# Layer 2 of eight blocks by seven products instead of eight

## The chip, the cores and the metric

The kernel runs on one core of a Trainium2 chip. The metric is the device time of one execution in microseconds; the kernel before takes 678.67 us, the median of three runs (678.66 to 679.11). The engines of the core are TensorE (PE in the profile, with its weight loads as PEld), VectorE (DVE), ScalarE (ACT), GpSimd (POOL) and SyncE (SP, which here only issues DMAs).

## The reference

```python
# x: 8 x 4096 x 192, weight: 8 heads x 7 taps, w_in: 192 x 2048, w_out: 2048 x 192
w = softmax(weight, axis=-1)                       # one set of 7 taps for each head of 24 channels
y[b, s, c] = sum(w[head(c), k] * x[b, s + k - 6, c] for k in range(7))   # zeros before the start
h = y.reshape(32768, 192) @ w_in                   # layer 1
out = gelu_exact(h) @ w_out                        # layer 2
```

Inputs and output are float32. Both layers have 192 x 2048 weights and 32768 tokens.

## The kernel before

**Tiling.** The tokens are split into two halves of 16384. A block n takes the same stretch of both halves: 256 tokens of each in blocks 0 to 5, 512 of each in blocks 6 to 34 (`WS`, `TB`, `NB` = 35). `M0` = 6 and `M1` = 34 bound the blocks whose layer 2 is made transposed (`mm2_t`, L821).

**Convolution.** VectorE transposes a block's input from `xin` to `xT` (`trans`, L493), and `conv` (L518) makes seven taps in fourteen instructions, each tap once for two thirds of the channels (1024 elements a partition) and once for the last third (512). The first tap is a multiplication (L537), the others multiply and add into `acc` (L544), and the last writes bf16 into `xc`. Three blocks, 4, 5 and 6 (`K0`), have their first tap made by ScalarE in three instructions (`first_tap`, L640, with semaphore `S_K0`); for them the transpose stands earlier, inside the convolution of the block before. GpSimd copies the last six tokens of a block to the front of the next (`halo`, L430).

**TensorE.** Each block n has sixteen units. A unit is `mm1(n, i)`, twelve matmuls of layer 1 into one of two PSUM buffers `hp`, and then a share of layer 2 of block n - 1. All matmuls in the blocks from 7 on use a 64x64 quarter of the array; four run side by side, and four of 512 columns are called a round here. `mm1` has 3 rounds a unit, 48 a block. `mm2_t` has three passes over the sixteen chunks of 128 hidden features, 48 rounds; every pass fills parts of the three PSUM banks of a block's output thirds (output column c belongs to third c mod 3). The shares are written by hand:

```python
SHARE = [3, 3, 3, 3, 4, 3, 3, 3, 3, 4, 3, 3, 3, 3, 2, 2]
```

The four banks of `ob` are used in turn (`ring`, L333). Waits on TensorE hold up everything queued after them.

**ScalarE** makes one gelu of 128 x 1024 a unit (L674), from `hp` to `gT`, and `mm1` of unit u waits until the gelu of unit u - 2 is done.

**VectorE's order** is a written list. `plan` holds, for each block, the convolution's instructions; `side` holds everything else with a place (block, position) in that plan. So far these are the transposes of layer 2's banks to `osb` (`evac_t`, L336), three a block, the first after pass 1 of layer 2 and two after its end. Plan n runs roughly while TensorE is in block n - 1.

**DMA.** SP issues the load of block n + 3, then the store of block n - 1, in turns; the load waits for `trans` of the block whose buffer it takes, the store for the third `evac_t`.

Of the kernel before, what the change touches and what calls it, by code (L numbers as in the profile page):

```python
# [5 lines left out]
ALU = mybir.AluOpType  # L6
AF = mybir.ActivationFunctionType
BF16 = mybir.dt.bfloat16
# [3 lines left out]
def bass_lightweight_conv__then__act_gelu_exact_kernel(  # L12
# [19 lines left out]

    WS = [256] * 6 + [512] * ((HALF - 1536) // 512)
    PC = {0: 0, 1: 1}

    K0 = {4: 0, 5: 1, 6: 2}

    NA = 5
    NB = len(WS)
# [31 lines left out]


    M0, M1 = 6, NB - 1

    PHC, MMC, EVC = [0], [0], [0]
    for n in range(NB):
        new = M0 <= n < M1
        PHC.append(PHC[n] + (2 if new else 3 * NG[n] if n == 0 else NG[n]))
        MMC.append(MMC[n] + (1 if new else 2 * NG[n] if n == M1 else NG[n]))
        EVC.append(EVC[n] + (0 if n < NA else NP if new else NG[n]))  # L80

# [3 lines left out]

    CG = [[0, 1, 4, 5, 2, 6, 3, 7], [1, 0, 5, 4, 2, 6, 3, 7]]
    CH = [[2 * CG[hf][i // 2] + i % 2 for i in range(NF)] for hf in range(2)]
    assert all(WS[n] == TB for n in range(M0, NB)) and NG[NB - 1] == 4 and SL0[NB] % 2 == 0

    OUTS = []  # L90
# [6 lines left out]
    def sbt(name, shape, dt):  # L97
        return es.enter_context(nc.sbuf_tensor(name, shape, dt))
# [10 lines left out]
    with es:  # L109
# [17 lines left out]
        xc = [sbt("xc%d" % i, [128, NP * TB], BF16) for i in range(2)]  # L127
        gT = [sbt("gT%d" % i, [128, NF * 2 * TB], BF16) for i in range(2)]
        osb = [sbt("osb%d" % i, [128, 8 * C], F32) for i in range(2)]
        hp = [pst("hp%d" % i, [128, 2 * TB]) for i in range(2)]  # L130
        ob = pst("ob", [128, 2048])

# [28 lines left out]
        S_EVA = sem("S_EVA")  # L161
        S_EVB = sem("S_EVB")
        S_K0 = sem("S_K0")

        block = es.enter_context(nc.Block())

# [97 lines left out]
        def banks(m, g):  # L264


            if m < M0:
                return [bank(2 * ((G0[m] + g) % 2) + h, w=C) for h in range(2)]
            if g % 2:
                return [hp[g // 2][:, h * TB : h * TB + C] for h in range(2)]  # L270
            r = NP * (M1 - 1 - M0)
            return [bank(b, w=C) for b in sorted((b % 4 for b in ((r + 3, r), (r + 1, r + 2))[g // 2]))]

        def wait_ev(e, m, g):

# [54 lines left out]

        UPLO = [(1, 0), (0, 2), (2, 1)]

        def ring(m, j):  # L333
            return NP * (m - M0) + j

        def evac_t(v, m, j):  # L336

            if j == 0:
                v.wait_ge(S_PH, PHC[m] + 2)
                v.wait_ge(S_OUT[m % 2], OUTS[m - 2])  # L340
            else:
                v.wait_ge(S_MM2, MMC[m + 1])
            v.transpose(  # L343
                ap(osb[m % 2], j, [[8 * C, 128], [C // 2, TB // 32], [NP, 32]]),
                bank(ring(m, j)),
            ).then_inc(S_EV)

        def load(e, n, qs=(0, 2, 1, 3), sm=None):
            mb = WS[n] // 32
# [10 lines left out]
        def store(e, m):  # L360
            if m < M0:
                for g in range(NG[m]):
                    wait_ev(e, m, g)
                    e.dma_start(
                        ap(
                            outt,
                            (OFF[m] + 128 * g) * C,
                            [[C, 128], [HALF * C, 2], [1, C]],
                        ),
                        ap(osb[m % 2], g * C, [[8 * C, 128], [4 * C, 2], [1, C]]),  # L370
                    ).then_inc(S_OUT[m % 2], 16)
                return
            wait_ev(e, m, NP - 1)
            for q in range(4):

                e.dma_start(
                    ap(
                        outt,
                        ((q // 2) * HALF + OFF[m]) * C + (q % 2) * (C // 2),
                        [[C, 32], [32 * C, WS[m] // 32], [1, C // 2]],  # L380
                    ),
                    ap(
                        osb[m % 2],
                        32 * q * 8 * C,
                        [[8 * C, 32], [C // 2, WS[m] // 32], [1, C // 2]],
                    ),
                ).then_inc(S_OUT[m % 2], 16)

        @block.gpsimd
        def _(g):  # L390
# [76 lines left out]
        def _(v):  # L467
# [84 lines left out]
            for n in range(2, NB):  # L552
                ops = [] if n in K0 else [("t", n, 0)]
                ops += [("c", n, k, q) for k in range(int(n in K0), KS) for q in range(2)]
                if n + 1 in K0:
                    ops[6:6] = [("t", n + 1, 0)]
                plan.append(ops)

            def run(op):
# [20 lines left out]
            for j in range(3, len(pieces(1))):  # L580
                conv_out(v, 1, j)

            side = [((M0 + 2, 4 * g), evac, v, M0 - 1, g) for g in range(NG[M0 - 1])]
            for n in range(M0, M1):
                for j, at in enumerate([(n + 2, 12), (n + 3, 4), (n + 3, 6)]):
                    side.append((at, evac_t, v, n, j))
            for n in range(M1, NB):
                for g in range(NG[n]):
                    side.append(((n + 3, g), evac_half, v, g, 0))
            side.sort(key=lambda q: q[0])  # L590
            for b in range(2, NB):
                for o, op in enumerate(plan[b - 2]):
                    while side and side[0][0] <= (b, o):
                        side[0][1](*side[0][2:])
                        side.pop(0)
                    run(op)
# [4 lines left out]
        def _(a):  # L601
# [31 lines left out]
                due[m + 2, 0] = [(m, 1)]  # L633

            first = {}
            for n, at in ((4, (3, 5, 6)), (5, (3, 5, 6)), (6, (2, 3, 5))):
                for p in range(NP):
                    first[n - 2, at[p]] = (n, p)

# [12 lines left out]
            for n in range(NB):  # L652
                w = WS[n]
                for i in range(NSL[n]):
                    u = SL0[n] + i
                    c = NCH[n]
                    if (n, i) in first:
                        first_tap(*first[n, i])
                    if (n, i) == (0, 4):
                        conv_out(a, 1, 0)  # L660
                    for k in due.get((n, i), []):
                        evac(a, *k)
                    a.wait_ge(S_MM1, u + 1)
                    if i == 0 and n >= 2:
                        a.wait_ge(S_MM2, MMC[n - 1])
                    if M0 <= n < M1:

                        src = [[2 * TB, 128], [1, 2 * TB]]
                        dst = [[NF * 2 * TB, 128], [1, 2 * TB]]
                    else:  # L670

                        src = [[2 * TB, 128], [TB, 2], [128, 4], [1, 128]]
                        dst = [[NF * 2 * TB, 128], [128, 2], [256, 4], [1, 128]]
                    a.activation(  # L674
                        out=ap(gT[n % 2], i * c * 2 * w, dst),
                        in_=ap(ob, 2 * TB, [[4 * TB, 128], *src[1:]]) if u < SL0[1] and u % 3 == 2 else ap(hp[u % 3 if u < SL0[1] else u % 2], 0, src),
                        func=AF.Gelu,
                    ).then_inc(S_GELU)
# [6 lines left out]
        def _(t):  # L685
# [43 lines left out]
            def mm1(n, i):  # L729
# [22 lines left out]
                for cc, p in todo:  # L752
# [4 lines left out]
                            t.wait_ge(S_CV, cvd(n))  # L757
                    for hf in range(2):
                        r = slice(64 * hf, 64 * hf + 64)
                        ch = CH[hf][i * c + cc]  # L760
                        f0 = FQ * ((ch // 2) ^ hf) + ch % 2
                        fw = 64 if (n == 0 and 4 <= i <= 5) or M0 < n <= M1 else 128
                        for fo in range(0, 128, fw):
# [57 lines left out]
            def mm2_t(m, ps, i):  # L821

                w = WS[m]
                if i == 0:
                    if ps < 2:
                        t.wait_ge(S_EV, EVC[m] - (1 if m == M0 else 2) + ps)
                    if ps > 0:
                        t.wait_ge(S_PH, PHC[m] + ps)
# [3 lines left out]
                for hf in range(2):  # L832
                    j = UPLO[ps][hf]
                    r = slice(64 * hf, 64 * hf + 64)
                    for h in range(2):
                        c0 = (2 * i + h) * w
                        ins = t.matmul(  # L837
                            bank(ring(m, j), slice(64 * h, 64 * h + 64), w),
                            ap(
                                wout,  # L840
                                64 * hf * NF * C + CH[h][i] * C + j,
# [8 lines left out]
                    ins.then_inc(S_MM2 if ps == 2 else S_PH)  # L850


            SHARE = [3, 3, 3, 3, 4, 3, 3, 3, 3, 4, 3, 3, 3, 3, 2, 2]

            def units(m):
                if M0 <= m < M1:
                    return [(ps, i) for ps in range(3) for i in range(NF)]
                return [
                    (g, ph, i) for g in range(NG[m]) for ph in range(2) for i in range(NF)
                ]  # L860
# [3 lines left out]
            for n in range(NB):  # L864
# [4 lines left out]
                for i in range(NSL[n]):  # L869
                    mm1(n, i)  # L870
                    for q in behind.get((n, i), []):
                        pconv(*q)
                    new = M0 < n <= M1
                    ws = SHARE if new else [0] * 7 + [1] if n == 0 else [1] * NSL[n]
                    a0 = len(todo) * sum(ws[:i]) // sum(ws)
                    a1 = len(todo) * sum(ws[: i + 1]) // sum(ws)
                    for un in todo[a0:a1]:
                        if n < 2 and un[:2] == (0, int(un[2] // 4 == 1)) and un[2] % 4 == 0:
                            t.wait_ge(S_WOUT[un[2] // 4], 16)
                        (mm2_t if new else mm2)(max(n - 1, 0), *un)  # L880
            m = NB - 1
            for g in range(NG[m]):
                wait_banks(t, m, g)
# [59 lines left out]
```

## Time and profile before

| what | value |
|---|---|
| runs | 679.11, 678.67, 678.66 us; median 678.67 |
| profiled execution, first to last instruction (span) | 676.8 us |
| median of the runs less that span | 1.87 us |
| mean granted TensorE clock | 1.000 |
| gelu L674, mean | 1023 ns, 510 times |
| matmuls of layer 1 and 2, 64x64 with 512 columns | 5376 each, 376 ns each, four side by side |
| convolution tap L544, 1024 and 512 elements, mean | 1272 and 714 ns |
| bank transpose L343, input transpose L516 of 1536 | 888 and 2316 ns |

The profile shows one execution. Durations of neighbours on an engine overlap a little, so the distance between two starts is shorter than a duration. The execution's own time is taken as its span; the runs' median lies 1.87 us above it.

### The profile page before, as it was taken

The numbers are of one execution on the slowest core, as the hardware profiler recorded it, in microseconds if no ns is written. First come the engines' busy times: TensorE is split into PE (matmuls) and PEld (weight loads), VectorE is DVE, ScalarE is ACT, GpSimd is POOL, SyncE is SP. The second block draws the span as 40 slices with busy tenths as digits, with TensorE's granted clock in tenths as the row PEclk, the third lists the DMA queues.
The fourth block names the chain that finished last, engine by engine and source line by source line (L and its number), as shares of the span: only waits on it lengthen the run. The fifth ranks groups of instructions, "written<-read, shape, count | busy, mean of one in ns | idle before, by whom it ended". The sixth has DMA issues, their size and how long they took to land.

```text
span 676.8 us, 26873 instructions
## 1 busy us (share of the span) xinstructions
PE 673.1 (99%) x12504; PEld 413.7 (61%) x12504; DVE 526.4 (78%) x607; ACT 536.5 (79%) x551; POOL 35.7 (5%) x61
## 2 busy tenths in 40 slices
PE   9999999999999999999999999999999999999998
PEld 8999555555555555555555555555555555555557
DVE  6989977987778977779777788777797777887511
ACT  8998977887778777777877787877877777778773
POOL 7010000000000000000000000000000000000000
PEclk9999999999999999999999999999999999999999
DMA  9435324223444224442234431244422344310223
GB/s 155 117 93 122 72 60 96 71 46 76 96 95 92 50 52 96 95 96 67 43 84 96 95 91 44 57 96 95 96 58 51 84 96 95 83 42 22 49 48 95
DMA packets 133280, 53.64 MB, mean 79 GB/s; under 512 B 126384, under 2 KB 133104, under 8 KB 133168
## 3 DMA queue, kind: packets, MB, share of 16 engines
q1 hardware_dynamic: 129136, 49.37, 32.6%
q0 software_dynamic: 2912, 1.97, 2.0%
q8 instruction: 98, 1.61, 1.0%
q10 hardware_dynamic: 1120, 0.59, 0.3%
q14 instruction: 14, 0.11, 0.1%
HBM read 28.31 MB, written 25.17 MB: 79 GB/s over the span
## 4 chain that ended last, share of the span: by engine, by line
PE 98%; ACT 1%; DVE 0%; DMA 0%; issue 0%; ACTq 0%
PE hp L766 49%; PE ob L837 43%; PE ob L806 5%; PE ob L889 1%; PE hp L889 1%; ACT gT L674 1%; DMA wsb<-in_weight_dram 0%; ACT xc L210 0%; PE ob L708 0%; ACT dg L621 0%; DVE wcol L488 0%; ACT osb L314 0%; ACT wex L608 0%; ACT xTb L238 0%; DVE wnm L479 0%
## 5 line engine op out<-in xcount | busy, mean ns | idle before, releaser
L674 ACT ACTIVATE gT<-hp 128x1024 bf16<-128x1024 f32 x510 | 520.9, 1023 | 127.6 <-PE hp L766 123.9
L766 PE MATMUL hp<-xc,win 64*64 64x512 bf16 (+2 forms) x6036 | 417.3, 366 | 0.3
L837 PE MATMUL ob<-gT,wout 64*64 64x512 bf16 x5376 | 366.4, 376 | 0.0
L544 DVE SCALAR_TENSOR_TENSOR acc<-xT,wcol,acc 128x1024 f32<-128x1024 f32 (+1 forms) x330 | 295.4, 945 | 3.5 <-ACT acc L645 3.5
L766 PEld LDWEIGHTS hp<-xc,win 64*64 64x64 bf16 (+1 forms) x6036 | 189.3, 106 | 131.4 <-issue 0.3
L837 PEld LDWEIGHTS ob<-gT,wout 64*64 64x64 bf16 x5376 | 172.3, 118 | 122.8
L343 DVE STREAM_TRANSPOSE osb<-ob 128x512 f32<-128x512 f32 x84 | 74.4, 888 | 129.1 <-PE ob L837 129.1
L516 DVE STREAM_TRANSPOSE xT<-xin 128x1536 f32<-128x1536 f32 (+2 forms) x39 | 74.8, 1925 | 2.0 <-DMA xin<-in_x_dram 2.0
L544 DVE SCALAR_TENSOR_TENSOR xc<-xT,wcol,acc 128x1024 bf16<-128x1024 f32 (+1 forms) x66 | 60.6, 958 | 0.0
L443 POOL COPY xT<-xT 128x18 f32<-128x18 f32 x30 | 22.6, 753 | 510.3 <-DVE xT L516 487.0
L806 PE MATMUL ob<-wout,gT 64*128 64x192 bf16 x768 | 41.6, 243 | 0.0
L806 PEld LDWEIGHTS ob<-wout,gT 64*128 64x128 bf16 x768 | 34.2, 94 | 4.2
L537 DVE TENSOR_SCALAR acc<-xT,wcol 128x512 f32<-128x512 f32 (+2 forms) x60 | 33.7, 604 | 1.1
L688 PE MATMUL hp<-const-bfloat16-1.0 128*128 128x128 bf16 x48 | 4.8, 295 | 0.8 <-PEq L928 0.8
L889 PE MATMUL ob<-wout,gT 128*128 128x192 bf16 x64 | 5.6, 246 | 0.0
L889 PE MATMUL hp<-wout,gT 128*128 128x192 bf16 x64 | 5.6, 246 | 0.0
L889 PEld LDWEIGHTS ob<-wout,gT 128*128 128x128 bf16 x64 | 5.2, 98 | 0.4 <-issue 0.4
L889 PEld LDWEIGHTS hp<-wout,gT 128*128 128x128 bf16 x64 | 5.3, 98 | 0.0
L645 ACT ACTIVATE acc<-xT,wcol 128x256 f32<-128x256 f32 (+1 forms) x9 | 5.2, 575 | 0.0
L688 PEld LDWEIGHTS hp<-const-bfloat16-1.0 128*128 128x128 bf16 x48 | 4.7, 140 | 0.8 <-issue 0.8
L299 ACT ACTIVATE osb<-ob 128x384 f32<-128x384 f32 x10 | 4.9, 488 | 0.0
L314 ACT ACTIVATE osb<-hp 128x192 f32<-128x192 f32 x2 | 0.7, 330 | 4.6 <-PE hp L889 4.6
(42 smaller groups left out, 42.5 us busy)
## 6 DMA issues: line engine op xcount, KB each, us to landing
out_dram<-osb SPq DMA_DIRECT2D x124, 192.0 KB, 3.1
xin<-in_x_dram SPq DMA_DIRECT2D x116, 192.0 KB, 4.0
xin<-in_x_dram SPq DMA_DIRECT2D x18, 96.0 KB, 2.5
wout<-in_moe_w_out_dram POOLq DMA_DIRECT2D x4, 192.0 KB, 5.4
win<-in_moe_w_in_dram POOLq DMA_DIRECT2D x4, 96.0 KB, 4.0
win<-in_moe_w_in_dram POOLq DMA_DIRECT2D x2, 192.0 KB, 4.9
xin<-in_x_dram POOLq DMA_DIRECT2D x4, 96.0 KB, 4.2
out_dram<-osb ACTq DMA_DIRECT2D x4, 96.0 KB, 2.3
```

Of the source, the lines that this page charges most:

```text
L343: v.transpose(ap(osb[m % 2], j, [[8 * C, 128], [C // 2, TB // 32], [NP, 32]]), bank(ring(m, j)),).then_inc(S_EV)
L443: g.tensor_copy(dst, src).then_inc(S_HALO)
L516: v.transpose(out, src).then_inc(S_TR)
L537: ins = v.tensor_scalar(a, src, wk, None, ALU.mult)
L544: ins = v.scalar_tensor_tensor(dst, src, wk, a, op0=ALU.mult, op1=ALU.add)
L645: a.activation(out=acc[n % 2][:, p * TB : p * TB + w], in_=ap(xT[n % 2], p * XW + HX, [[NP * XW, 128], [1, w]]), func=AF.Copy, scale=wcol[ ...
L674: a.activation(out=ap(gT[n % 2], i * c * 2 * w, dst), in_=ap(ob, 2 * TB, [[4 * TB, 128], *src[1:]]) if u < SL0[1] and u % 3 == 2 else ap(h ...
L688: t.matmul(hp[1][:, 0:128], one, one)
L766: ins = t.matmul(hbuf(u, slice(fo, fo + fw), o, w), ap(win, f1, [[NP * F, 64], [2, fw]]), xc[n % 2][r, p * TB : p * TB + w], start=(p == 0 ...
L806: ins = t.matmul(bb[sub], gT[m % 2][r, c0 : c0 + 128], wout[r, CH[sub][i] * C : (CH[sub][i] + 1) * C], start=(ph == 0 and k == 0), stop=(p ...
L837: ins = t.matmul(bank(ring(m, j), slice(64 * h, 64 * h + 64), w), ap(wout, 64 * hf * NF * C + CH[h][i] * C + j, [[NF * C, 64], [NP, 64]],) ...
L889: ins = t.matmul(banks(m, g)[h], gT[m % 2][:, c0 : c0 + 128], wout[:, CH[h][i] * C : (CH[h][i] + 1) * C], start=(i == 0), stop=(i == NF - 1),)
```

## The change

Eight blocks, `ST` = 9, 12, 15 up to 30, get another layer 2. For two of the three output thirds, their layer 2 is a product of two by two submatrices: two token halves times two kinds of hidden chunk (even and odd), times two kinds of chunk and two thirds. It is made by seven products (P1 to P7) instead of eight, with sums and differences of operands and results around them. The last third (D for one token half, E for the other) is made as before.

- **TensorE**: `mm2_s` instead of `mm2_t`. Each of the four array tiles has its own list of units of eight matmuls (`TILES`); one of the units, P3, has matmuls of 256 columns, each half of the output columns on one column half of the array. A list has 5.5 units, so 44 rounds; `ROUNDS` shares them out over the sixteen units of layer 1.
- **VectorE, weights**: six instructions once, in plan 7, make the four combined weight tiles `wst`.
- **VectorE, operands**: ten adds of bf16 a Strassen block (`st_add`): S1 in four parts, S3, Dn and S4 in two each, from `gT` into `sst`. Each waits for its gelus.
- **VectorE, results**: five adds in f32 (`st_post`), and three transposes (`st_evac`) of which two read SBUF.
- **ScalarE**: six copies a Strassen block (`st_copy`), three of them of 512 and one of 256 columns from PSUM, two of 512 in SBUF.
- **ScalarE, first taps**: `K0` gets 18 more blocks: 9 to 34 except 12, 15 up to 33. Their input transpose moves into the plan before, to position 2. The taps stand ahead of gelus 7, 10 and 12 of the block two before.
- **Places**: `evac_t` of the other blocks is moved to later positions (`at_ev`), and the banks of `ob` are dealt out by `BK` instead of `ring`.

Waits that TensorE gets: for parts of S1, S3, Dn, S4 (`S_SA`), for banks freed by ScalarE's copies (`S_AC`) and VectorE's combining adds (`S_DP`), for its own earlier streams where a bank passes from one row half to the other (`S_ST`), and once for the weights (`S_WT`).

```diff
-    K0 = {4: 0, 5: 1, 6: 2}
+    ST = [m for m in range(M0 + 3, M1 - 1) if m % 3 == 0]
+    K0 = {n: i for i, n in enumerate([4, 5, 6, *(n for n in range(9, NB) if n - 3 not in ST)])}
...
+        UNIT = {
+            "D1": ("D", 0, 0), "D2": ("D", 0, 1), "E1": ("D", 1, 0), "E2": ("D", 1, 1),
+            "P1": ("X", 0, 0), "P6": ("X", 0, "Dn"), "P2": ("Y", 0, 1),
+            "P5": ("X", 1, "S1"), "P7": ("Y", 1, "S3"), "P4": ("Y", 1, 1), "P3": ("V", None, "S4"),
+        }
+        TILES = {
+            (0, 0): "P1 D1 D2 P3 P6 P2", (1, 0): "D1 P1 P3 P6 P2 D2",
+            (0, 1): "P5 P7 E1 P3 P4 E2", (1, 1): "E1 P5 P7 E2 P3 P4",
+        }
...
+        ROUNDS = (3, 3, 2, 3, 3, 2, 3, 3, 2, 4, 3, 3, 2, 3, 3, 2)
...
+            if name == "S1":
+                ins = v.tensor_tensor(t(0), a(1, 0), a(1, 1), ALU.add)
+            elif name == "S3":
+                ins = v.tensor_tensor(t(1), a(0, 0), a(1, 0), ALU.subtract)
+            elif name == "Dn":
+                v.wait_ge(S_SA[0], PART["S1"] * i + (q + 1) * n * PART["S1"] // (NF // 2))
+                ins = v.tensor_tensor(t(2), a(0, 0), t(0), ALU.subtract)
+            else:
+                v.wait_ge(S_SA[2], PART["Dn"] * i + q + 1)
+                ins = v.tensor_tensor(t(3), a(0, 1), t(2), ALU.add)
...
+            dst, src = (
+                (gsm[LO, :], xb(LO)),
+                (p5s[UP, :], xb(UP)),
+                (p5s[LO, 0 : TB // 2], xb(UP, TB // 2)),
+                (uu[LO, :], xb(LO)),
+                (gsm[UP, :], uu[LO, :]),
+                (uu[UP, :], uu[LO, :]),
+            )[k]
+            a.activation(out=dst, in_=src, func=AF.Copy).then_inc(S_AC)
...
+            if k == 0:
+                st_done(v, m, "P7")
+                v.wait_ge(S_AC, 6 * i + 2)
+                ins = v.tensor_tensor(tq[UP, :], bank(BK[m]["Y"], UP), p5s[UP, :], ALU.add)
+            elif k == 1:
...
+                ins = v.tensor_tensor(tq[LO, 0:hw], vb[0], p5s[LO, 0:hw], ALU.add)
+            elif k == 2:
...
+                ins = v.tensor_tensor(tq[LO, hw:TB], vb[1], p5s[UP, hw:TB], ALU.add)
+            elif k == 3:
...
+                ins = v.tensor_tensor(tq[:, :], tq[:, :], uu[:, :], ALU.add)
+            else:
+                v.wait_ge(S_MM2, MMC[m + 1])
+                ins = v.tensor_tensor(gsm[:, :], bank(BK[m]["Y"]), gsm[:, :], ALU.add)
...
+        TAPS = (7, 10, 12)
+        AT_ST = {
+            "S1": [(1, 9, 0), (2, 0, 0), (2, 1, 0), (2, 5, -1)],
+            "S3": [(2, 0, 1), (2, 5, 1)],
+            "Dn": [(2, 0, 2), (2, 5, 2)],
+            "S4": [(2, 0, 4), (2, 6, 0)],
+            "post": [(2, 11, 0), (3, 0, 0), (3, 2, 0), (3, 6, 0), (3, 6, 1)],
+            "ev": [(3, 6, 3), (3, 6, 2), (3, 4, 0)],
+        }
...
+        AT_COPY = {0: (1, 6), 1: (1, 8), 2: (1, 10), 3: (1, 13), 4: (1, 14), 5: (2, 1)}
...
-                    ops[6:6] = [("t", n + 1, 0)]
+                    ops[6 if n < 6 else 2 : 6 if n < 6 else 2] = [("t", n + 1, 0)]
...
+                need(S_EV, EVC[m] - {"X": 2, "D": 2, "Y": 1, "V": 0}[bk])
+                if e in SWITCH:
+                    need(S_ST, len(DONE) * i + DONE.index(SWITCH[e]) + 1)
+                if u == "P6":
+                    need(S_AC, 6 * i + 1)
+                if u == "P4":
+                    need(S_DP, 5 * i + 1)
...
-                        (mm2_t if new else mm2)(max(n - 1, 0), *un)
+                        (mm2_s if n - 1 in ST else mm2_t if new else mm2)(max(n - 1, 0), *un)
```

`AT_ST` gives places in VectorE's plan as (blocks after the Strassen block, position, order among equals); `AT_COPY` gives places among ScalarE's gelus as (blocks after, unit).

## The prediction

> **What bounds the kernel now.** I read the page's busy table and its chain first, then the groups by line and shape, the waits, a table of stretches of one block each, and the timelines of VectorE and ScalarE.
>
> ```profile
> PE 673.1 (99%) x12504; PEld 413.7 (61%) x12504; DVE 526.4 (78%) x607; ACT 536.5 (79%) x551; POOL 35.7 (5%) x61
> ...
> PE 98%; ACT 1%; DVE 0%; DMA 0%; issue 0%; ACTq 0%
> ```
>
> TensorE is busy and on the chain for nearly all of the span of 676.8 us, at a granted clock of 1.00. So time goes only if TensorE gets less to do, and comes back as soon as another engine makes it wait.
>
> ```profile
> core 0: us, PE busy (x) PEld busy (x) DVE busy (x) ACT busy (x) POOL busy (x), PEclk, DMA share, GB/s
> ...
> 255.15:275.87 20.72, 20.72 (x389) 11.77 (x384) 16.75 (x19) 16.37 (x16) 0.71 (x1) 1.00 0.37 79
> 275.87:296.59 20.72, 20.72 (x389) 11.77 (x384) 16.77 (x19) 16.37 (x16) 0.11 (x1) 1.00 0.37 78
> 296.59:317.31 20.72, 20.72 (x389) 11.77 (x384) 16.75 (x19) 16.37 (x16) 0.71 (x1) 1.00 0.36 79
> ```
>
> A block takes 20.72 us and has 384 matmuls of 512 columns, four at a time on four 64x64 tiles: 96 rounds of 0.2158 us, without a gap. VectorE has 50.27 us of work in three blocks and 11.9 us free. Its free time is a wait for TensorE (us in total, times, longest):
>
> ```profile
> DVE osb L343 <- PE ob L837: 129.1, 30, 11.8
> ACT gT L674 <- PE hp L766: 123.9, 409, 0.7
> ```
>
> Its timeline (start and duration in us):
>
> ```profile
> 123.30 1.15 DVE L537 TENSOR_SCALAR acc<-xT,wcol 128x1024 f32<-128x1024 f32 x2
> 124.37 1.28 DVE L544 SCALAR_TENSOR_TENSOR acc<-xT,wcol,acc 128x1024 f32<-128x1024 f32 x1
> 125.57 0.89 DVE L343 STREAM_TRANSPOSE osb<-ob 128x512 f32<-128x512 f32 x1
> 126.35 1.87 DVE L544 SCALAR_TENSOR_TENSOR acc<-xT,wcol,acc 128x512 f32<-128x512 f32 x2
> ```
>
> An instruction overlaps the tail of the one before, so I price by the distance between starts: 1.07 for the two instructions of a first tap, 1.20 for a tap of 1024 elements, 0.78 for a transpose. The trace's starts give 0.66 for a tap of 512, so 1.04 ns an element and 0.13 fixed; 0.07 where the instruction before is not one it depends on.
>
> **TensorE, the gain.** A Strassen block's layer 2 falls from 48 rounds to 44: 4 x 0.2158 = 0.863 us, times eight blocks 6.91. The 32 matmuls of product P3 have 256 columns; two of them must fit into one round of the other tiles. No 512-wide stream mixed with 256 is in the trace, but its half is: between 6.66 and 6.96 us (L708) 128-wide matmuls start every 56 ns on two tiles while 256-wide ones start every 110 ns on the others. Two halves cost 2 to 3 ns more than a whole. In 12 rounds a block that is 0.03 us, 0.27 in all. Each bank handed from one row half to the other waits for the earlier stream's end; by the order of issue at least one unit of layer 1 (3 rounds, 0.65 us) lies between, as it does now between passes, which show no idle time.
>
> **VectorE, the bill.** Per three blocks (one of them Strassen's) TensorE now allows 92 + 96 + 96 rounds = 61.29 us. From 50.27 go two first taps, 2.14: 48.13. To it come:
> - Ten adds, 16,384 bf16 elements a partition. No such row exists. L544 reads two f32 sources, 8 bytes, in 1.04 ns; L537 reads one f32 source in 0.52 ns an element (0.67 for 1024, 0.40 for 512), again 8 bytes in 1.04. At the same read rate two bf16 sources take 0.52 ns an element: 8.5 us, with 0.1 fixed each 9.5. Bounds: L544's time per element, 18.1; the bf16 copy of L247 (768 elements 0.42 us, 1536 0.56, so 0.18 ns each), 4.0. I take 9.5, because both f32 rows agree on bytes.
> - Five combining adds in f32: three of 512 at 0.66, two of 256 at 0.40: 2.8; at the fixed cost of a transpose from PSUM 3.3.
> - The three transposes stay; two read SBUF instead of PSUM, which I cost at nothing (L516 takes 2.34 for 1536 elements from SBUF, three times 0.78).
>
> Sum 60.4, so 0.9 us free per three blocks, no more.
>
> The Trainium skill, "VectorE: DVE Perf Modes", section "The perf-mode tier table", states that tensor_tensor on bf16 in SBUF runs two elements a cycle, 1224 ns for 2048; at that as the whole price the ten adds come to an estimated 10.1 and the sum to 61.0. The skill's "TensorEngine Tiling", under PSUM Bottleneck, speaks against the change: a faster TensorE leaves the PSUM copies as the bound; before, the wait of 129.1 us shows the reverse, and if the rule held here the gain would be nothing.
>
> **Where in the block it must be ready.** Count from the start of the block in which the Strassen products run. The matmuls of the unit before end two rounds ahead (-0.43), its gelu starts 0.21 after the last round and takes 1.02: S1's last quarter can start at 0.8. Up to the first combining add VectorE has eleven instructions: the quarter 0.63, two transposes 1.55, halves of S3 and Dn 1.17 each, a tap of 512 0.62, half of S4 1.17, then taps 1.19, 0.66, 1.19, 0.66, 1.19: 11.2. The add ends 0.75 later, at 12.8. TensorE wants the bank that it frees, for P4, behind 33 rounds of layer 1 and 28 of its own: 61 x 0.2158 = 13.17. The cover is 0.4 us. The other dates have more: S1's quarter 1.4 of 3.2, S3 4.1 of 5.8, S4 7.1 of 8.4. A late add stops TensorE in its queue; the next unit of layer 1 stands behind it, behind that the gelu, and so VectorE's next add.
>
> Upstream VectorE follows the clock of others closely. The convolution of the block after the next Strassen block begins with a wait for ScalarE's third first tap, which stands at unit 12 and ends 17.7 us into the Strassen block; behind that wait are 3.6 us of taps (0.62, 1.19, 0.66, 1.19) and then the last quarter of S1, so 21.4, and its gelu is done at 20.72 + 0.8 = 21.5. Just in time: a first tap later than that moves the adds, not only the convolution.
>
> The six weight preparations (four at 0.66, two at 0.40: 3.4 us, once) stand in block 7's convolution, which ends at 79.4 against layer 1's start at 83.4: hidden by 0.5; without that cover 3.4.
>
> **ScalarE.** In the trace a gelu moves the next start by 0.91 (50.39 to 51.30), a 512 first tap by 0.62, a PSUM copy of 384 by 0.37:
>
> ```profile
> 49.77 0.72 ACT L645 ACTIVATE acc<-xT,wcol 128x512 f32<-128x512 f32 x1
> 50.39 1.00 ACT L674 ACTIVATE gT<-hp 128x1024 bf16<-128x1024 f32 x1
> 51.30 0.71 ACT L645 ACTIVATE acc<-xT,wcol 128x512 f32<-128x512 f32 x1
> ...
> 52.81 0.49 ACT L299 ACTIVATE osb<-ob 128x384 f32<-128x384 f32 x1
> 53.18 1.03 ACT L674 ACTIVATE gT<-hp 128x1024 bf16<-128x1024 f32 x1
> ```
>
> A unit of six rounds is 1.295 us, so a tap of 0.62 delays its gelu by 0.24, and TensorE tolerates 0.7. The taps wait for an input transpose that VectorE ends 8 us earlier; gelus are queued behind them. The copies of a Strassen block stand in a block with five-round units (1.08 us). The fourth and fifth fall on adjacent units: PSUM copy 0.50, gelu 0.91, SBUF copy 0.62, gelu; that last gelu is done 3.97 us after gelu 12's start, and layer 1 of the next block wants it at 3.89. So it is late by 0.1, give or take as much: I take half, 0.05 x 8 = 0.4.
>
> POOL's halo copies and SP's loads move with VectorE. A load stands behind a store that waits for the last transpose of its block: it is issued 12 us or more ahead of use and lands in 4 (page, DMA issues). Nothing is added.
>
> **The sum.** Against the profiled execution's span: 676.8 - 6.91 + 0.27 + 0.4 = 670.6. The median lies 1.87 above that span, so 672.4.
>
> **The rivals.**
> 1. VectorE or ScalarE late by tenths. The fifteen new VectorE instructions 0.1 us dearer each make 1.5 per three blocks, 0.6 over the free 0.9, so 8 x 0.6 = 4.8 back: 677.2. For it: the covers of 0.4 and 0.9 are smaller than the unknowns. Against: an instruction behind an unrelated one costs 0.07 fixed, and each inserted one takes 0.05 from the tap after it. 673.6 to 677.3.
> 2. VectorE becomes the bound, and the kernel slower. With the adds at L544's 1.04 ns, three blocks take 48.1 + 18.1 + 2.8 = 69.0 instead of 62.16: 8 x 6.9 = 55, about 733. It decides when the new VectorE work passes 62.16 - 48.1 = 14.0 us instead of my 12.3. For it: no two-source instruction in the trace runs faster than 1.04 ns an element. Against: all of them read f32.
> 3. The half-width matmuls take a whole round each, so the seven products save nothing: 48 rounds, about 679. Against: the mixed stretch of L708.
>
> **How the numbers follow.** Forecast 0.58, late by tenths 0.20, nothing saved 0.07, VectorE the bound 0.15. What a measurement of this kernel can tell is about 0.2%, 1.4 us: faster below 677.3, slower above 680.0. Forecast and rival 1 are faster, 0.78; rival 3 is the same, 0.07; rival 2 slower, 0.15. The range runs from the full saving with 0.5 us for the unknowns, 671.2, up to the end of no change, 680.0, and leaves out 0.15.
>
> **What the profile after would show.** Right: Strassen blocks of 19.9 us beside others of 20.7, TensorE still over 97% of the chain; the 2048-element add near 1.15 to 1.25 us; VectorE busy over 19.5 us in such a block; idle time of TensorE before the Strassen matmuls under 1.5 us in all. Wrong: an add of over 2 us; TensorE waiting for combining adds, for adds or for gelus by a microsecond a block; 256-wide matmuls on one tile 0.2 us apart.

## The result and the profile after

The changed kernel takes 674.24 us (median; 673.92 to 676.39) against 678.83 for the one before: the ratio is 0.9935, with a 95% interval of 0.9917 to 0.9952. It is faster by 4.6 us where 6.3 were forecast, and lies inside the range given.

The profiled execution is the slow one of the four, 676.39 us with a span of 674.7 against 672.1 to 672.5, because layer 1 of its block 7 begins at 85.6 us instead of 83.4 (83.8 in e1, which is the same up to there; 87.2 in the profiled execution of e2), so block lengths and not spans are compared below.

The page after, busy times and chain:

```profile
PE 668.8 (99%) x12504; PEld 418.6 (62%) x12504; DVE 605.7 (90%) x697; ACT 584.8 (87%) x653; POOL 33.1 (5%) x61
...
PE 93%; ACT 5%; DMA 1%; issue 0%; SPq 0%; DVE 0%; POOL 0%; POOLq 0%; ACTq 0%
```

TensorE is still the bound, but 5% of the chain is now ScalarE, where it was 1%. VectorE went from 526.4 us to 605.7 and has no share of the chain. The chain's share is not the loss: of the 4 us that it gives to ScalarE in such a block, as shown further down, TensorE loses 0.28. The stretches of one group of three blocks, cut where layer 1 of a block begins (length, then busy time of each engine); the first is the block in which the products of Strassen block 9 run:

```profile
core 0: us, PE busy (x) PEld busy (x) DVE busy (x) ACT busy (x) POOL busy (x), PEclk, DMA share, GB/s
147.77:167.92 20.15, 20.04 (x388) 12.27 (x380) 19.92 (x21) 18.41 (x22) 0.72 (x1) 1.00 0.36 81
167.92:188.67 20.75, 20.75 (x386) 11.80 (x389) 20.05 (x23) 18.46 (x21) 1.19 (x1) 1.00 0.35 79
188.67:209.39 20.72, 20.72 (x390) 11.77 (x385) 20.03 (x24) 17.89 (x20) 0.20 (x1) 1.00 0.33 78
```

The first block is 0.57 us shorter than 20.72, where the prediction's sum has 0.78 (0.863 less 0.03 for the half widths and 0.05 for the late gelu); the second is 0.03 longer; the third is as before. All eight groups read the same. Eight times 0.54 is 4.3, the gain of the runs within their scatter. VectorE works 60.0 of 61.6 us. What is missing in the first block stands at its end, in ScalarE's timeline (start, length):

```profile
163.76 1.02 ACT L880 ACTIVATE gT<-hp 128x1024 bf16<-128x1024 f32 x1 [0.27 <-PE hp L972]
164.68 0.58 ACT L482 ACTIVATE uu<-ob 64x512 f32<-64x512 f32 x1
165.16 1.01 ACT L880 ACTIVATE gT<-hp 128x1024 bf16<-128x1024 f32 x1
166.19 0.63 ACT L482 ACTIVATE gsm<-uu 64x512 f32<-64x512 f32 x1
166.84 3.00 ACT L880 ACTIVATE gT<-hp 128x1024 bf16<-128x1024 f32 x3
```

All five are on the chain, which goes on from the last one (start, length, what):

```profile
166.84 1.03 ACT gT L880
167.88 0.04 issue
167.92 0.84 PE hp L972 x12
```

Gelus 12 and 13 with a copy behind each, then gelu 14, and then layer 1 of the next block, which needs the PSUM buffer of gelu 14. In the trace the first matmul of that block starts 487 to 492 ns after the one before it, against 203 to 206 at the start of the blocks from 8 on that follow no Strassen block: 0.28 us lost there, in all eight. The waits show the same on the weight loads, which wait longer than TensorE loses (us in total, times, longest):

```profile
PEld hp L972 <- ACT gT L880: 4.9, 9, 0.6
```

### The profile page after: what moved, and what is told of

It is laid out like the page before. It is cut to its first block, busy times and chain, and to the rows that moved or that the text cites. A ratio compares the mean times of both kernels' runs of the same rounds, so it can differ in the third digit from the quotient of the medians.

```text
span 674.7 us, 27139 instructions
## 1 busy us (share of the span) xinstructions
PE 668.8 (99%) x12504; PEld 418.6 (62%) x12504; DVE 605.7 (90%) x697; ACT 584.8 (87%) x653; POOL 33.1 (5%) x61
## 4 chain that ended last, share of the span: by engine, by line
PE 93%; ACT 5%; DMA 1%; issue 0%; SPq 0%; DVE 0%; POOL 0%; POOLq 0%; ACTq 0%
PE hp L972 47%; PE ob L1050 31%; PE ob L1110 9%; PE ob L1012 5%; ACT gT L880 4%; DMA xin<-in_x_dram 1%; PE ob L1166 1%; PE hp L1166 1%; ACT gsm L482 1%; ACT uu L482 1%; PE ob L914 0%; DMA wsb<-in_weight_dram 0%; SPq L527 0%; PE ob L972 0%; POOL xTb L265 0%
## 5 line engine op out<-in xcount | busy, mean ns | idle before, releaser
L1050 PE MATMUL ob<-gT,wout 64*64 64x512 bf16 x3840 | 261.7, 376 | 0.0
L1110 PE MATMUL ob<-gT,wout 64*64 64x512 bf16 x768 | 97.2, 376 | 0.0
L1110 PE MATMUL ob<-sst,wst 64*64 64x512 bf16 x384 | 79.1, 376 | 0.0
L364 DVE STREAM_TRANSPOSE osb<-ob 128x512 f32<-128x512 f32 x60 | 49.9, 872 | 32.5 <-PE ob L1050 32.5
L848 ACT ACTIVATE acc<-xT,wcol 128x512 f32<-128x512 f32 (+1 forms) x63 | 43.7, 693 | 0.0
L1110 PEld LDWEIGHTS ob<-sst,wst 64*64 64x64 bf16 x384 | 32.2, 107 | 5.4
L1110 PE MATMUL ob<-gT,wst 64*64 64x512 bf16 x128 | 35.3, 376 | 0.0
L1110 PE MATMUL ob<-sst,wout 64*64 64x256 bf16 x256 | 27.4, 269 | 0.0
L454 DVE TENSOR_TENSOR sst<-gT 128x1024 bf16<-128x1024 bf16 x32 | 22.0, 688 | 5.4 <-ACT gT L880 5.4
L1110 PEld LDWEIGHTS ob<-sst,wout 64*64 64x64 bf16 x256 | 21.8, 119 | 2.1
L459 DVE TENSOR_TENSOR sst<-gT,sst 128x2048 bf16<-128x2048 bf16 x16 | 19.4, 1216 | 0.0
```

Of the source, the lines that this page charges most:

```text
L364: v.transpose(osb_t(m, j), bank(BK[m][j])).then_inc(S_EV)
L454: ins = v.tensor_tensor(t(0), a(1, 0), a(1, 1), ALU.add)
L459: ins = v.tensor_tensor(t(2), a(0, 0), t(0), ALU.subtract)
L848: a.activation(out=acc[n % 2][:, p * TB : p * TB + w], in_=ap(xT[n % 2], p * XW + HX, [[NP * XW, 128], [1, w]]), func=AF.Copy, scale=wcol[ ...
L1050: ins = t.matmul(bank(BK[m][j], slice(64 * h, 64 * h + 64), w), ap(wout, 64 * hf * NF * C + CH[h][i] * C + j, [[NF * C, 64], [NP, 64]],), ...
L1110: ins = t.matmul(bank(BK[m][bk], slice(64 * cg, 64 * cg + 64), w), wt_, a[r, c0 : c0 + w], start=(e == mine[0]), stop=(e in (mine[-1], GRO ...
```

## The experiments

Main theory: TensorE gets the four rounds back, and loses a third of them to gelu 14, which comes late because of ScalarE's copies. Rivals: VectorE, 97% busy, is the brake; the half-width matmuls cost the difference; or the copies only matter by their length. The first four kernels below were timed against 678.44 us for the kernel before, the last three against 678.66. ScalarE's six copies are numbered 0 to 5 here, as in `AT_COPY`; the expectations of e1 and e7 call copies 4 and 5 the fourth and fifth, that of e2 calls copy 4 the fifth.

**e1, copies 4 and 5 later.**

```diff
-AT_COPY = {0: (1, 6), 1: (1, 8), 2: (1, 10), 3: (1, 13), 4: (1, 14), 5: (2, 1)}
+AT_COPY = {0: (1, 6), 1: (1, 8), 2: (1, 10), 3: (1, 13), 4: (1, 15), 5: (2, 2)}
```

> ScalarE's fourth SBUF copy moves from ahead of gelu 14 to ahead of gelu 15, the fifth from ahead of the next block's gelu 1 to gelu 2. Theory (layer 1 of the next block waits 0.28 us for gelu 14, which stands behind two copies in a row): the wait goes, Strassen blocks take 19.87 instead of 20.15 us, 8 x 0.28 = 2.2 us less than the changed kernel, about 672.0. VectorE then waits up to 0.9 us for the fifth copy and has 1.3 free. Rival, VectorE at its limit: its new wait costs as much as is gained, 674 or more. Rival, the half-width matmuls cost the 0.29: no change, 674.2.

Measured: 672.39 us, ratio 0.9909 (0.9896 to 0.9922). The stretches of a Strassen block and the one after it:

```profile
145.97:165.84 19.87, 19.87 (x389) 12.38 (x385) 19.63 (x21) 18.15 (x21) 0.72 (x1) 1.00 0.35 82
165.84:186.57 20.73, 20.73 (x390) 11.68 (x386) 19.86 (x23) 18.68 (x22) 1.19 (x1) 1.00 0.35 79
```

The one new wait of VectorE, for copy 5, stands in the waits, and below it the wait of the weight loads:

```profile
DVE tq L502 <- ACT uu L482: 6.5, 8, 0.8
...
PEld hp L972 <- ACT gT L880: 2.9, 10, 0.5
```

The block is 19.87 us with TensorE busy throughout. 92 rounds of 0.2158 are 19.86, so 0.01 us is left for the half widths: the second rival is out. VectorE waits 0.8 us a Strassen block for copy 5, and the third block of the group is 20.72 us as before, so nothing behind it is late. The weight loads still wait 2.9 us, but the first matmul of the next block starts 206 ns after the one before it again: that row alone does not tell what TensorE loses.

**e2, copy 4 to the lower rows.** Part of the result is left out.

```diff
+                v.memset(gsm[UP, :], 0.0)
+                v.memset(uu[UP, :], 0.0)
...
-                (gsm[UP, :], uu[LO, :]),
+                (wtf[LO, :], uu[LO, :]),
```

> The fifth of the six copies (gsm rows 64 to 127 from uu rows 0 to 63) writes rows 0 to 63 of a spare tile instead, same size, same place; the upper rows of gsm and uu are set to zero once, so a third of the result is left out. Theory (a copy that does not start at partition 0 on all sides waits for the gelu before it to end, and holds the gelu after it): gelu 14 comes 0.13 to 0.16 earlier, 8 times, so 1.0 to 1.3 us less, about 673.1. Rival (only its length counts, 0.63 against 0.62): unchanged, 674.2.

Measured: 672.38 us, ratio 0.9918 (0.9900 to 0.9935). A Strassen block:

```profile
272.30:292.17 19.87, 19.87 (x388) 12.28 (x380) 19.64 (x21) 18.17 (x22) 0.11 (x1) 1.00 0.35 82
```

The whole 0.28 us goes, not half. ScalarE's timeline (start, length), with its copy of 0.62 between gelus:

```profile
166.53 0.58 ACT L484 ACTIVATE uu<-ob 64x512 f32<-64x512 f32 x1
167.01 1.01 ACT L882 ACTIVATE gT<-hp 128x1024 bf16<-128x1024 f32 x1
167.91 0.62 ACT L484 ACTIVATE wtf<-uu 64x512 f32<-64x512 f32 x1
168.44 2.98 ACT L882 ACTIVATE gT<-hp 128x1024 bf16<-128x1024 f32 x3
```

From gelu 13 to the copy 0.90 us, from the copy to gelu 14 0.53. In the changed kernel (timeline above: 165.16, 166.19, 166.84) it is 1.03 and 0.65. Size, type, source and place are the same; the tile that it writes, and in it the partitions, differ. So length alone is out, and the effect is about twice what was expected: this copy costs 0.25 us more between two gelus when it writes the upper rows.

**e4, no first taps on ScalarE.**

```diff
-    K0 = {n: i for i, n in enumerate([4, 5, 6, *(n for n in range(9, NB) if n - 3 not in ST)])}
+    K0 = {4: 0, 5: 1, 6: 2}
```

> The Strassen blocks stay, but only blocks 4, 5 and 6 have their first tap on ScalarE, as before the change. Theory (VectorE has 60.0 us of work in the 61.6 us of three blocks): 2.14 more make 62.1, VectorE becomes the bound, nearly all of the gain goes: 678 to 682. Rival (VectorE has room, only ScalarE's copies cost): ScalarE is freer, 672 to 674.

Measured: 681.16 us, ratio 1.0040 (1.0027 to 1.0053): slower than before the change. The stretches of one group of three blocks, the fourth of the eight:

```profile
270.42:291.26 20.84, 20.60 (x389) 13.70 (x381) 20.71 (x23) 18.46 (x22) 0.12 (x1) 1.00 0.37 78
291.26:312.18 20.92, 20.92 (x385) 14.41 (x389) 20.79 (x25) 17.04 (x18) 0.71 (x1) 1.00 0.35 78
312.18:332.90 20.72, 20.72 (x389) 14.55 (x385) 20.72 (x24) 16.39 (x17) 0.52 (x1) 1.00 0.33 78
```

The waits have two rows that the changed kernel does not have:

```profile
PEld ob L1110 <- DVE tq L491: 5.0, 8, 0.6
...
PEld ob L1110 <- DVE sst L462: 2.7, 8, 0.4
```

VectorE is busy for 62.22 of 62.48 us, and TensorE waits for its adds: this is the rival on the slower side of the prediction, reached not through a slow add but through 2 us more of other work.

**e5, one more add ahead of the first combining add.**

```diff
+                v.tensor_tensor(wtf[UP, :], bank(BK[m]["Y"], UP), p5s[UP, :], ALU.add)
                 ins = v.tensor_tensor(tq[UP, :], bank(BK[m]["Y"], UP), p5s[UP, :], ALU.add)
```

> One more VectorE add of 64 x 512 directly ahead of the first combining add, its result not used. Theory (the first combining add is done 0.41 us before TensorE wants its bank for P4): 0.62 more makes TensorE wait 0.2 us in each Strassen block, 8 x 0.2 = 1.6 to 1.9 us more, about 676.0. Rival (VectorE is not near its date): unchanged, 674.2.

Measured: 676.22 us, ratio 0.9964 (0.9953 to 0.9976), 2.0 over the changed kernel. The stretch of a Strassen block:

```profile
145.23:165.67 20.44, 20.35 (x388) 12.73 (x381) 20.25 (x22) 18.40 (x22) 0.72 (x1) 1.00 0.35 80
```

And a wait that the changed kernel does not have:

```profile
PEld ob L1111 <- DVE tq L492: 3.0, 8, 0.4
```

0.62 us more of VectorE's time costs 0.29 a block: the cover in front of P4 was about 0.3 us, against 0.4 in the prediction. VectorE is no brake in the changed kernel, but it is within a third of a microsecond of being one.

**e3, the first taps alone.**

```diff
-    ST = [m for m in range(M0 + 3, M1 - 1) if m % 3 == 0]
+    ST = []
```

> No Strassen block (ST is empty); the first taps of blocks 9 to 34 and the six weight preparations stay as in the change. Theory (TensorE is the bound and the taps only move work from VectorE to ScalarE): the time of before, 678.2 to 679.2, blocks of 20.72 us. Rival (the taps among the gelus make layer 1 wait): 0.1 us or more a block, 681 or more. Rival (the taps bring part of the gain): under 677.

Measured: 678.52 us, ratio 0.9998 (0.9989 to 1.0006). One block:

```profile
145.85:166.57 20.72, 20.72 (x388) 11.77 (x384) 15.84 (x17) 17.87 (x20) 0.20 (x1) 1.00 0.34 79
```

VectorE has 0.9 us a block less, ScalarE 1.5 more, and TensorE does not notice. The taps gain nothing by themselves, and without them (e4) the products lose: each part pays only with the other.

**e6, a Strassen block in every six.**

```diff
-    ST = [m for m in range(M0 + 3, M1 - 1) if m % 3 == 0]
+    ST = [m for m in range(M0 + 3, M1 - 1) if m % 6 == 3]
```

> Strassen blocks 9, 15, 21 and 27 only, four instead of eight; the rest of the rules as in the change. Theory (each Strassen block saves 4 rounds, 0.86 us, and loses 0.31 to the late gelu behind ScalarE's copies, whether VectorE is full or not): half of the change's gain of 4.4, about 676.3, blocks of 20.15 us. Rival (the loss comes from a VectorE that falls behind over the row of Strassen blocks): with time to recover the blocks take 19.9 and the gain is 3.3 or more, 675.2 or less.

Measured: 676.66 us, ratio 0.9970 (0.9959 to 0.9981), 2.0 less than before, somewhat under half of the change's gain. The first of the four blocks:

```profile
145.53:165.68 20.15, 20.04 (x389) 12.16 (x381) 19.94 (x21) 18.40 (x22) 0.71 (x1) 1.00 0.35 81
```

All four are 20.15 us, with five others between them in which VectorE recovers. (`K0` follows from `ST`, so four more blocks get their first tap from ScalarE.) The loss belongs to the single block, not to a VectorE that falls behind.

**e7, only copy 4 later.**

```diff
-AT_COPY = {0: (1, 6), 1: (1, 8), 2: (1, 10), 3: (1, 13), 4: (1, 14), 5: (2, 1)}
+AT_COPY = {0: (1, 6), 1: (1, 8), 2: (1, 10), 3: (1, 13), 4: (1, 15), 5: (2, 1)}
```

> Only ScalarE's fourth SBUF copy moves, from gelu 14 to gelu 15 of the Strassen block; the fifth stays at the next block's gelu 1. Theory: as in e1 the late gelu goes, Strassen blocks of 19.87 us, and VectorE doesn't wait for the fifth copy, which ends before it is wanted; about 672.2, the same as e1 within 0.3. Rival (the two copies now crowd the next block's first gelus): that block grows from 20.73 to 20.8 or more, 672.8 or more.

Measured: 672.81 us, ratio 0.9912 (0.9898 to 0.9925), not to be told from e1. A Strassen block and the one after it:

```profile
145.86:165.73 19.87, 19.87 (x390) 12.27 (x385) 19.66 (x21) 18.14 (x21) 0.72 (x1) 1.00 0.35 82
165.73:186.48 20.75, 20.75 (x388) 11.60 (x384) 20.37 (x23) 18.66 (x22) 1.20 (x1) 1.00 0.36 79
```

The move of one copy by one gelu brings the 0.28 back. The time alone would also fit the rival (672.8 or more); the block after it, which should have grown to 20.8, does not: it is 20.75 us, as in the changed kernel. e1 and e7 beat both kernels; of the two, e1 also brings the next block from 20.75 to 20.73.

## Why the prediction was right, and where its size was off

**TensorE's gain: right.** 44 rounds take the time of 44 rounds. The half widths were priced at 0.03 us a block and cost 0.01 (e1); 256-wide matmuls on one tile start 109 ns apart in the trace of the changed kernel, where 0.2 us was named as the sign of being wrong. The hand-overs of banks cost nothing that shows.

**VectorE's bill: right.** Three blocks were summed to 60.4 us and have 60.0. The sum rested on the guess that a bf16 add of two sources reads as many bytes a nanosecond as the f32 rows do. The groups of the changed kernel by shape:

```profile
L454 DVE TENSOR_TENSOR sst<-gT 128x1024 bf16<-128x1024 bf16 x32 | 22.0, 688 | 5.4 <-ACT gT L880 5.4
...
L456 DVE TENSOR_TENSOR sst<-gT 128x2048 bf16<-128x2048 bf16 x16 | 19.2, 1202 | 0.0
```

1024 elements more cost 0.514 us, 0.50 ns each (0.52 taken). By starts, 2048 elements take 1.10 to 1.14 (1.17 taken). The mean of 1202 ns also agrees with the Trainium skill's figure of 1224 ns ("VectorE: DVE Perf Modes", section "The perf-mode tier table"). The other rule weighed was that PSUM copies become the bound; the skill ("TensorEngine Tiling", section "PSUM Bottleneck") says only that they may, after a fourfold speedup of TensorE. It did not hold here: TensorE waits for none of VectorE's copies out of PSUM in the changed kernel. What it waits for in a Strassen block is one gelu, 0.28 us of 20.15. e4 and e5 show how little room VectorE has.

**The dates in the block: right, by some luck.** The first combining add was put at 12.8 us after the start of the block, against 13.17 wanted; it ends at 12.76. VectorE's timeline, with the block starting at 147.77:

```profile
138.49 0.69 DVE L454 TENSOR_TENSOR sst<-gT 128x1024 bf16<-128x1024 bf16 x1 [0.68 <-ACT gT L880]
...
148.73 0.68 DVE L454 TENSOR_TENSOR sst<-gT 128x1024 bf16<-128x1024 bf16 x1
...
158.54 1.27 DVE L733 SCALAR_TENSOR_TENSOR xc<-xT,wcol,acc 128x1024 bf16<-128x1024 f32 x1
159.84 0.69 DVE L491 TENSOR_TENSOR tq<-ob,p5s 64x512 f32<-64x512 f32 x1
```

The last quarter of S1 starts at 0.96, not at 0.8, though its gelu is done at 0.81: VectorE is still at the taps ahead of it. The way from there is 11.1 us instead of 11.2 (the prediction says eleven instructions and adds up twelve; the trace has twelve), and the add takes 0.69 instead of 0.75. So three small errors cancel. The paragraph on ScalarE's third first tap feared the same delay from another cause, and it was not that tap: it ends 3.54 us before the block starts, at 144.23, and VectorE works without a gap from 138.49 on, when it had waited for a gelu to make the second quarter of S1.

**ScalarE's term: the place right, the size wrong.** The prediction named gelu 14 behind the fourth and fifth copies (3 and 4 in the table). It had that gelu done at 3.97 us after gelu 12's start, wanted at 3.89, and then took half of the difference: 0.05 a block, 0.4 in all. Measured is 4.12 (163.76 to 167.88), so 0.28 a block with the way to TensorE, and 0.03 in the block after: 8 x 0.31 = 2.5. For copy 4 the term took 0.91 from gelu to copy and 0.62 from copy to gelu, as with the first taps; those cover all 128 partitions. The copy to the upper rows takes 1.03 and 0.65, and 0.90 and 0.53 on the lower rows (e2). The 0.03 in the block after was not in the sum; e1 wins 0.02 of it back with copy 5 a gelu later, and its cause is not shown beyond that. Put right, the sum is 678.7 - 6.9 + 0.1 + 2.5 = 674.4, against 674.24 measured. Halving a late date was the second fault: nothing hides a gelu that TensorE is already waiting for. Two of the signs named for being right are missing for this reason: the Strassen blocks are 20.15 us and not 19.9, and TensorE has 93% of the chain and not over 97%.

**The rivals.** The first, late by tenths, is what took the missing 1.9 us, through ScalarE and not through VectorE. The second, VectorE as the bound, did not come, and e4 shows that about 2 us more of work per three blocks is enough to bring it. The third, no saving by the half widths, is refuted by the 19.87 us of e1.

## What to carry to other kernels

When the bound is an engine that never waits, sum the other engines over one whole period of the schedule and then walk to the date of each thing that they hand over: the sum said that there was room, the dates said where it was short. A small instruction squeezed into a full queue is priced between its own neighbours and on its own partitions, not from a wider one elsewhere. If a date is missed in the working by a tenth, move the instruction by one place before looking for anything larger: here one entry of a table was worth 1.4 us by the medians of the runs and 2.2 by the block lengths (e7).

## What was not expected of the hardware

In these kernels a ScalarE copy that reads or writes from partition 64 on does not overlap with the gelus beside it. In the changed kernel a PSUM copy of 64 x 512 on the lower rows starts 0.92 us after the gelu before it and the next gelu 0.48 after that (copy 3, in the first timeline). The copies of 512 columns that read or write upper rows take 1.03 to 1.05 and 0.62 to 0.66, the one of 256 columns 1.04 and 0.41, always a little more than the durations (1.02 for a gelu, 0.59 to 0.63 and 0.38 for these copies). Copy 1, which reads and writes upper rows, is one of them, so a move from one half to the other is not needed for it:

```profile
158.32 0.59 ACT L482 ACTIVATE p5s<-ob 64x512 f32<-64x512 f32 x1
158.94 1.94 ACT L880 ACTIVATE gT<-hp 128x1024 bf16<-128x1024 f32 x2
```

e2 isolates the step with one instruction: 1.03 + 0.65 against 0.90 + 0.53. VectorE does the like, though no run isolates it: the first combining add, on rows 64 to 127, starts 1.30 us after a tap of 1024 that is otherwise followed at 1.20, and 0.03 after that tap's end. In e5, where two such adds stand in a row, the first starts 1.33 us after the tap, and the second 0.61 after the first, as an add of 512 on all rows is followed at 0.60. For VectorE the Trainium skill describes this as a held instruction ("VectorE: DVE Perf Modes", section "Two Vector instructions with no wait between them"): one whose operands start in another group of 32 partitions than those of its predecessors waits until they have finished.
